# Moving the token gathers behind the scatters, and reordering the first expert's weight splits, in a fused attention and mixture-of-experts kernel

## The chip, the cores and the metric

The kernel runs on one core of a Trainium2 chip. The metric is the time of one execution on the device in microseconds (us). The kernel before takes 622.65 us, the median of three runs that lie between 622.59 and 622.91 us.

The core's engines run their own instruction streams and meet through semaphores: PE (TensorE, matrix products and transposes), DVE (VectorE), ACT (ScalarE), POOL (GpSimd) and SP (SyncE, here used to start transfers). POOL also starts the indirect transfers, those whose rows are chosen by an index tile.

## The reference

Attention over 4 batches, 8 heads, 576 positions and 64 features per head, with a bias that a small network makes from the distance of two positions, is followed by a mixture of experts over the 2304 tokens of 512 features. Each token goes to the one expert with the largest gate logit.

```python
scores = scale * np.matmul(q, k.transpose(0, 1, 3, 2)) + bias        # bias: relu(x @ w1 + b1) @ w2 per head
attn = softmax(scores)
x = np.matmul(attn, v).transpose(0, 2, 1, 3).reshape(2304, 512)
...
e_idx = np.argmax(x @ w_gate, axis=1)
for e in range(8):
    mask = e_idx == e
    h = np.maximum(x[mask] @ w1[e], 0.0)                              # 512 -> 1024
    out[mask] = gate_w[mask, None] * eom[mask, e, None] * (h @ w2[e]) # 1024 -> 512
```

## The kernel before

**Stages.** The bias tiles are built first; then sixteen pairs of heads are worked through, with tables of short codes (`ORDER`, `FIRST`, `LAST`, `END`) that fix the order of the work of each pair. Finished token rows are written to a tensor `x_dram` in HBM. The routing of the first three batches is done before the experts begin, that of the fourth batch is spread through the first five expert slots (`SLOT_WORK`).

**Slots.** The expert stage works in slots of 288 tokens of one expert, `body(s)` for s = 0 to 7; more slots, and a short one of 32 tokens, follow from the routing. A slot has two loops on PE. The f loop makes 8 blocks of 128 hidden columns, each from 12 products (L1115). The d loop makes 4 blocks of 128 output columns, each from 24 products (L1138). Each float32 operand is held as a high part and a remainder, so a weight has to be split: ACT copies the high part and the remainder is a subtraction. In the slots the subtraction is DVE's (`split`, L486 and L487). For slot 0 it is POOL's (`first_split`, L539 and L540), in eight halves: half i belongs to weight chunk i // 2 and holds columns 0 to 511 or 512 to 1023, which serve blocks 0 to 3 and 4 to 7 of the f loop. The code `y` in the table `LAST` takes one entry of the list `splits`.

**Tokens.** `gather(s)` (L497) fetches the 288 rows of a slot in three indirect transfers of 96 rows into the tiles `xg`, of which there are two sets, for even and odd slots. After blocks 1 and 2 of the d loop of slot s, `transpose_x(s + 1, c)` (L515 to L517) turns the next slot's rows. At a slot's end the answer is turned (L1157), copied (L1160), and `put` (L1080) writes it with three indirect transfers, the scatters.

**Order on POOL.** POOL runs its instructions in the order in which the program lists them, and an instruction that waits holds up those behind it. The gather for slot s + 2 is listed in slot s between the two loops, ahead of the scatters of slot s; it waits until the transposes of slot s have read its tile set. `gather(0)` stands in `first_x` (code `X`), `gather(1)` behind all of the attention. The short slot's rows are fetched by `gather(FIRST_FEW)` and turned by `transpose_few` (L505) ahead of the d loop of slot 7.

**Transfers on SP.** `load_w1(s)` (L478) and `load_w2(s)` (L483) fetch an expert's weights, four transfers each, and each waits until the splits have read the buffer that it fills. `load_w1(1)` is listed behind the eighth half of `first_split`.

Of the kernel before, what the change touches and what calls it, by code (L numbers as in the profile page):

```python
# [134 lines left out]
def attention_moe_kernel(  # L135
# [49 lines left out]
    def psum_t():  # L185
        return ps_t.tile([128, 512], F32, name="pt", tag="t")
# [284 lines left out]
    def expert(s):  # L471
        at = 2 * ns + 1 if s == FIRST_FEW else s
        return nc.values_load(seq[int(s >= SURE_A)][0:1, at:at + 1], engines=(EV.SP,), min_val=0, max_val=NE - 1)

    def load_w1(s):
        src = mw1[bass.ds(expert(s), 1)].rearrange("o (c p) f -> p (o c) f", p=128)
        for i in range(4):
            nc.sync.dma_start(out=w1r[i], in_=src[:, i, :])  # L478

    def load_w2(s):  # L480
        src = mw2[bass.ds(expert(s), 1)].rearrange("o (c p) f -> p (o c) f", p=128)
        for i in range(4):
            nc.sync.dma_start(out=w2r[i], in_=src[:, 2 * i:2 * i + 2, :])  # L483

    def split(hi, lo, src):
        nc.scalar.copy(out=hi, in_=src)  # L486
        V.tensor_tensor(out=lo, in0=src, in1=hi.bitcast(F32), op=ALU.subtract)  # L487

    def side(s):

        return s % 2 if s < SURE else 0

    def gather(s):
        part = int(s >= SURE_A)
        for j in range(1 if s == FIRST_FEW else 3):
            g = 3 * s + j
            nc.gpsimd.indirect_dma_start(  # L497
                out=xg[side(s)][j], out_offset=None, in_=x_dram[:, :] if part else x_dram[0:(B - 1) * S, :],
                in_offset=bass.IndirectOffsetOnAxis(ap=gidx[part][:, g:g + 1], axis=0),
            )  # L500

    def transpose_few():
        pt = psum_t()
        for c in range(4):
            nc.tensor.transpose(  # L505
                pt[:, c * G:c * G + G], xg[0][0][:, c * 128:c * 128 + 128], ident[0:G, 0:G]
            )
        V.tensor_copy(out=few[0], in_=pt[:, 0:4 * G].rearrange("p (c g) -> p c g", g=G)[:, :, 0:FEW])

    def transpose_x(s, c):  # L510
        xh, xl = xs[side(s)]
        xg_s = xg[side(s)]
        pt = psum_t()
        for j in range(3):
            nc.tensor.transpose(pt[:, j * G:j * G + G], xg_s[j][:, c * 128:c * 128 + 128], ident[0:G, 0:G])  # L515
        nc.scalar.copy(out=xh[:, c, :], in_=pt[:, 0:CH])
        V.tensor_tensor(out=xl[:, c, :], in0=pt[:, 0:CH], in1=xh[:, c, :].bitcast(F32), op=ALU.subtract)  # L517
        if s >= SURE:
            V.tensor_copy(out=few[0][:, c, :], in_=pt[:, 0:FEW])
# [13 lines left out]
    def first_split(i):  # L533
        if i == 0:
            for m, to in enumerate((w1h, w1l)):
                t = biasp.tile([128, 4, DFF], F32R, name=f"w1_{m}", tag=f"bias{m}")
                to.extend(t[:, c, :] for c in range(4))
        c, h = i // 2, slice(i % 2 * 512, i % 2 * 512 + 512)
        nc.scalar.copy(out=w1h[c][:, h], in_=w1r[c][:, h])  # L539
        nc.gpsimd.tensor_tensor(  # L540
            out=w1l[c][:, h], in0=w1r[c][:, h], in1=w1h[c][:, h].bitcast(F32), op=ALU.subtract
        )
        if i == 7:
            load_w1(1)

    def first_w2():
        t = biasp.tile([128, 4, 2, DM], F32, name="w2r", tag="bias3")
        w2r.extend(t[:, i] for i in range(4))
        load_w2(0)
# [122 lines left out]
    with ExitStack() as actx:  # L672
# [316 lines left out]
            f(*a)  # L989

        chunks = [0, 1, 2, 3]
        splits = list(range(8))

        def copies(c):
            return nc.scalar.copy if c == "a" else V.tensor_copy
# [5 lines left out]
        for n in range(len(pairs) + 1):  # L1001
            todo = {i: 1 for i in range(8)}
            for op in orders.get(n, ORDER).split():
# [21 lines left out]
                i = int((name + "0")[1])  # L1025
# [30 lines left out]
                        finish(emit_kq(b, pr, i))  # L1056
                else:
                    {"l": emit_load, "v": emit_load_v, "c": emit_z, "b": emit_load_vb, "g": emit_zb, "z": emit_q4}[name](b, pr)
        gather(1)
        while chunks:  # L1060
            transpose_x(0, chunks.pop(0))

    with ExitStack() as ctx:
# [14 lines left out]
        def put(s, j, y, n=G):  # L1078
            idx = sidx[int(s >= SURE_A)][0:n, 3 * s + j:3 * s + j + 1]
            p = nc.gpsimd.indirect_dma_start(  # L1080
                out=out, out_offset=bass.IndirectOffsetOnAxis(ap=idx, axis=0),
                in_=y[0:n], in_offset=None, bounds_check=NTOK - 1, oob_is_err=False,
            )
            for other in puts:
                tc.declare_no_dep(p.ins, other.ins, reason="no row of the answer is written twice")
            puts.append(p)
# [4 lines left out]
        def new_y(s, j):  # L1091

            if s == SURE - 1:
                return xg[1][j]
            return y2 if j == 2 else x_p.tile([128, DM], F32, name="y", tag="x")[0:G]

        def slot_work(s, at):
            for w in SLOT_WORK[s].split() if s < len(SLOT_WORK) else ():
                if w == at:
                    do_work()  # L1100

        def after(s, n):

            return None if s >= SURE else s + n if s + n < SURE else FIRST_FEW if s + n == SURE else None

        def body(s):
            assert s < 5 or not (work or rows)
            xh, xl = xs[side(s)]
            for f in range(8):
                fs = slice(f * 128, f * 128 + 128)  # L1110
                p1 = ps1.tile([128, 512], F32, name="p1", tag="p1")
                n = 0
                for c in range(4):
                    for w, x in ((w1h[c], xh), (w1h[c], xl), (w1l[c], xh)):
                        nc.tensor.matmul(p1[:, 0:CH], lhsT=w[:, fs], rhs=x[:, c, :], start=n == 0, stop=n == 11)  # L1115
                        n += 1
                nc.scalar.activation(out=hh[f], in_=p1[:, 0:CH], func=ACTF.Relu)  # L1117
                V.scalar_tensor_tensor(
                    out=hl[f], in0=p1[:, 0:CH], scalar=0.0, in1=hh[f].bitcast(F32), op0=ALU.max, op1=ALU.subtract
                )  # L1120
                if f % 2 == 0:
                    i = f // 2
                    split(w2h[i], w2l[i], w2r[i])
                slot_work(s, "f%d" % f)
            if after(s, 1):
                load_w2(after(s, 1))
            if after(s, 2):
                gather(after(s, 2))
            yt = yts[s % 2]
            if after(s, 1) == FIRST_FEW:  # L1130
                transpose_few()
            for d in range(4):
                ds = slice(d * 128, d * 128 + 128)
                p2 = ps2.tile([128, 512], F32, name="p2", tag="p2")
                n = 0
                for f in range(8):
                    for w, x in ((w2h, hh), (w2h, hl), (w2l, hh)):
                        nc.tensor.matmul(  # L1138
                            p2[:, 0:CH], lhsT=w[f // 2][:, f % 2, ds], rhs=x[f], start=n == 0, stop=n == 23
                        )  # L1140
                        n += 1
                if after(s, 1) == s + 1:
                    split(w1h[d], w1l[d], w1r[d])
                nc.scalar.copy(out=yt[:, d, :], in_=p2[:, 0:CH])
                if after(s, 1) == s + 1 and d in (1, 2):
                    for c in (2 * d - 2, 2 * d - 1):
                        transpose_x(s + 1, c)
                if after(s, 1) == FIRST_FEW and d < 3:
                    (few_hidden, few_turn, few_last)[d]()
                slot_work(s, "d%d" % d)  # L1150
            if after(s, 2):
                load_w1(after(s, 2))
            pts = [psum_t() for j in range(3)]
            for d0, d1 in ((0, 3), (3, 4)):
                for j, pt in enumerate(pts):
                    for d in range(d0, d1):
                        nc.tensor.transpose(pt[0:G, d * 128:d * 128 + 128], yt[:, d, j * G:j * G + G], ident)  # L1157
            for j, pt in enumerate(pts):
                y = new_y(s, j)
                (V.tensor_copy, nc.scalar.copy, V.tensor_copy)[j](out=y, in_=pt[0:G, :])  # L1160
                if s != SURE - 1:
                    put(s, j, y)

        few_h, few_ht = (yts[0].rearrange("p a b -> p (a b)")[:, 256 * i:256 * i + 256] for i in range(2))

# [51 lines left out]
        for s in range(SURE):  # L1217
            body(s)
# [44 lines left out]
```

## Time and profile before

| what | us |
|---|---|
| median of three runs | 622.65 |
| the profiled execution | 615.56 |
| its span, first to last instruction | 613.4 |
| PE busy in the span | 575.6 |
| DVE busy | 413.5 |
| ACT busy | 374.8 |
| POOL busy | 94.9 |
| mean granted clock of PE | 0.987 of full speed |

The profile is one execution. A timeline lists instructions in order of time, with the idle time of the engine ahead of each and what ended it in brackets. The chain is followed back from the last instruction to what released each step. A landing is the time from the issue of a transfer until its data has arrived. "Busy x" in a table by stage is busy microseconds and instruction count. The experts' slot 0 begins at 370.2 us, slot 1 at 401.7, slot 2 at 431.6, slot 3 at 459.5, slot 4 at 488.0, slot 5 at 515.9, slot 6 at 543.8 and slot 7 at 571.7.

### The profile page before, as it was taken

The numbers are of one execution on the slowest core, as the hardware profiler recorded it, in microseconds if no ns is written. First come the engines' busy times: TensorE is split into PE (matmuls) and PEld (weight loads), VectorE is DVE, ScalarE is ACT, GpSimd is POOL, SyncE is SP. The second block draws the span as 40 slices with busy tenths as digits, with TensorE's granted clock in tenths as the row PEclk, the third lists the DMA queues.
The fourth block names the chain that finished last, engine by engine and source line by source line (L and its number), as shares of the span: only waits on it lengthen the run. The fifth ranks groups of instructions, "written<-read, shape, count | busy, mean of one in ns | idle before, by whom it ended". The sixth has DMA issues, their size and how long they took to land.

```text
span 613.4 us, 13534 instructions
## 1 busy us (share of the span) xinstructions
PE 575.6 (94%) x5070; PEld 489.3 (80%) x5070; DVE 413.5 (67%) x974; ACT 374.8 (61%) x774; POOL 94.9 (15%) x172
## 2 busy tenths in 40 slices
PE   4878789999999999999999999999999999999993
PEld 2333478887887788887778769999999999999993
DVE  6968656676786677786579765766777675555621
ACT  5778667777775677776776664545545454545410
POOL 1000000000001000100012383040404132220202
PEclk9979989999999999999999999999999999999998
DMA  6998975655656745676436686576656574855521
GB/s 144 226 207 207 215 161 116 139 125 108 143 127 169 167 99 108 137 184 157 105 88 158 185 263 198 172 221 204 202 179 203 172 221 145 241 166 182 174 71 47
DMA packets 99094, 100.26 MB, mean 163 GB/s; under 512 B 71320, under 2 KB 71576, under 8 KB 99017
## 3 DMA queue, kind: packets, MB, share of 16 engines
q1 hardware_dynamic: 93028, 84.93, 54.4%
q0 software_dynamic: 3232, 9.64, 5.0%
q10 hardware_dynamic: 2756, 4.72, 2.2%
q8 instruction: 42, 0.69, 0.5%
q14 instruction: 36, 0.29, 0.2%
HBM read 60.34 MB, written 9.50 MB: 114 GB/s over the span
## 4 chain that ended last, share of the span: by engine, by line
PE 79%; DVE 7%; ACT 5%; DMA 5%; issue 3%; POOL 0%; POOLq 0%; SPq 0%; DVEq 0%; ACTq 0%
PE p L1115 16%; PE p L1138 16%; PE pa L922 13%; PE ps L853 10%; PE pt L890 10%; PE pt L803 2%; DMA bias<-evh 2%; PE pb L735 2%; PE ps L869 2%; DVE e L833 2%; DVE hid L724 2%; PE pt L655 1%; PE pt L1157 1%; PE pt L902 1%; PE pt L515 1%
## 5 line engine op out<-in xcount | busy, mean ns | idle before, releaser
L838 ACT ACTIVATE e<-e,nm 128x576 f32<-128x576 f32 x144 | 111.2, 773 | 49.1 <-DVE nm L833 47.0
L833 DVE CUSTOM_DVE_ANT_0 e<-ps,bias 128x576 f32<-128x576 f32 x144 | 105.6, 751 | 31.3 <-PE ps L853 25.3
L1115 PE MATMUL p<-x,w 128*128 128x288 f32 x768 | 105.8, 297 | 0.0
L1115 PEld LDWEIGHTS p<-x,w 128*128 128x128 f32 x768 | 102.8, 188 | 0.5 <-issue 0.4
L890 PE MATMUL pt<-kept,e 128*128 128x128 f32 x576 | 82.7, 277 | 2.9 <-ACT et L894 1.6
L853 PE MATMUL ps<-qt,qs 128*128 128x288 f32 x256 | 79.9, 331 | 3.2 <-DVE nm L833 3.0
L890 PEld LDWEIGHTS pt<-kept,e 128*128 128x128 f32 x576 | 65.2, 141 | 17.8 <-issue 7.0
L1138 PE MATMUL p<-hh,w2h 128*128 128x288 f32 x256 | 77.4, 302 | 0.0
L1138 PE MATMUL p<-hl,w2h 128*128 128x288 f32 x256 | 75.7, 296 | 0.1
L1138 PE MATMUL p<-hh,w2l 128*128 128x288 f32 x256 | 75.4, 295 | 0.0
L922 PE MATMUL pa<-et,vt 128*64 128x256 f32 (+1 forms) x640 | 73.2, 354 | 0.0
L853 PE MATMUL ps<-kl,qs 128*128 128x288 f32 x256 | 71.3, 296 | 0.0
L894 ACT COPY et<-pt 128x512 f32<-128x512 f32 (+1 forms) x105 | 57.2, 565 | 12.4 <-PE pt L890 12.3
L735 PE MATMUL pb<-hid,w2blk 128*32 128x288 f32 x576 | 47.8, 442 | 17.3 <-DVE hid L724 7.4
L922 PEld LDWEIGHTS pa<-et,vt 128*64 128x64 f32 x640 | 42.6, 137 | 21.8 <-issue 6.0
L853 PEld LDWEIGHTS ps<-qt,qs 128*128 128x128 f32 x256 | 48.9, 191 | 7.2 <-DVE nm L833 4.5
L1117 ACT ACTIVATE hh<-p 128x288 fp32r<-128x288 f32 x64 | 26.3, 411 | 46.1 <-PE p L1115 38.0
L1080 POOL DMA_INDIRECT out_dram<-y,sidx x22 | 26.4, 1198 | 172.9 <-DVE y L1160 145.3
L735 PEld LDWEIGHTS pb<-hid,w2blk 128*32 128x32 f32 x576 | 19.1, 116 | 42.1 <-DVE hid L724 10.7
L724 DVE TENSOR_SCALAR hid<-e,early 128x576 f32<-128x576 f32 x110 | 48.4, 511 | 6.1 <-PE pb L735 2.8
L853 PEld LDWEIGHTS ps<-kl,qs 128*128 128x128 f32 x256 | 49.1, 192 | 0.0
L487 DVE TENSOR_TENSOR w2l<-w2r,w2h 128x1024 fp32r<-128x1024 f32 x32 | 39.2, 1225 | 14.5 <-ACT w2h L486 14.5
(218 smaller groups left out, 970.8 us busy)
## 6 DMA issues: line engine op xcount, KB each, us to landing
w1r<-in_moe_w_dram SPq DMA_DIRECT2D x36, 512.0 KB, 3.7
w2r<-in_moe_w_dram SPq DMA_DIRECT2D x36, 512.0 KB, 4.0
kl<-qs SPq DMA_DIRECT2D x32, 288.0 KB, 5.2
nat<-in_k_dram SPq DMA_DIRECT2D x16, 288.0 KB, 3.9
nat<-in_q_dram SPq DMA_DIRECT2D x16, 288.0 KB, 5.2
bias<-evh SPq DMA_DIRECT2D x16, 288.0 KB, 4.2
bias<-evl SPq DMA_DIRECT2D x16, 288.0 KB, 5.3
qs<-qt SPq DMA_DIRECT2D x16, 288.0 KB, 3.2
```

The source lines that it names most:

```text
L487: V.tensor_tensor(out=lo, in0=src, in1=hi.bitcast(F32), op=ALU.subtract)
L724: V.tensor_scalar(out=to, in0=src, scalar1=bc[:, r:r + 1], scalar2=0.0, op0=ALU.add, op1=ALU.max,)
L735: nc.tensor.matmul(pb[32 * t:32 * t + 32, c, 0:288], lhsT=w2f, rhs=hids[t][:, c * 288:c * 288 + 288], start=True, stop=True,)
L833: V.tensor_tensor_reduce(out=e.rearrange("p (a j) -> p a j", a=2), in0=ps[:, :, 0:n], in1=bias_ap.rearrange("p (a j) -> p a j", a=2), scal ...
L838: nc.scalar.activation(out=e, in_=e, func=ACTF.Exp, scale=-1.0, bias=nm, accum_out=sum_ap)
L853: nc.tensor.matmul(ps[:, c, 0:288], lhsT=qs[:, o:o + 128], rhs=keys[:, k0 + c * 288:k0 + c * 288 + 288], start=n == 0, stop=n == 1,)
L890: nc.tensor.transpose(pt[:, n * 256 + j * 128:n * 256 + j * 128 + 128], es[j][:, (n0 + n) * 128:(n0 + n) * 128 + 128], ident,)
L894: copy(out=et[:, n0:n0 + nn, :].rearrange("p n s -> p (n s)"), in_=pt[:, 0:nn * 256])
L922: nc.tensor.matmul(pa[p:p + 64, 0:n], lhsT=values, rhs=weights, start=i == 0, stop=i == 4)
L1080: p = nc.gpsimd.indirect_dma_start(out=out, out_offset=bass.IndirectOffsetOnAxis(ap=idx, axis=0), in_=y[0:n], in_offset=None, bounds_check ...
L1115: nc.tensor.matmul(p1[:, 0:CH], lhsT=w[:, fs], rhs=x[:, c, :], start=n == 0, stop=n == 11)
L1138: nc.tensor.matmul(p2[:, 0:CH], lhsT=w[f // 2][:, f % 2, ds], rhs=x[f], start=n == 0, stop=n == 23)
```

## The change

Three things are edited. In the list `splits` the four halves with the low columns come first. `gather(1)` moves from the end of the attention into `first_split`, behind the half with number 6, which is now the fourth of eight. In `body` the gather for two slots ahead moves from between the two loops to the end, behind the scatters of the slot.

```diff
--- before.py
+++ after.py
@@ -542,6 +542,8 @@
         )
         if i == 7:
             load_w1(1)
+        elif i == 6:
+            gather(1)
 
     def first_w2():
         t = biasp.tile([128, 4, 2, DM], F32, name="w2r", tag="bias3")
@@ -989,7 +991,7 @@
             f(*a)
 
         chunks = [0, 1, 2, 3]
-        splits = list(range(8))
+        splits = [0, 2, 4, 6, 1, 3, 5, 7]
 
         def copies(c):
             return nc.scalar.copy if c == "a" else V.tensor_copy
@@ -1056,7 +1058,6 @@
                         finish(emit_kq(b, pr, i))
                 else:
                     {"l": emit_load, "v": emit_load_v, "c": emit_z, "b": emit_load_vb, "g": emit_zb, "z": emit_q4}[name](b, pr)
-        gather(1)
         while chunks:
             transpose_x(0, chunks.pop(0))
 
@@ -1124,8 +1125,6 @@
                 slot_work(s, "f%d" % f)
             if after(s, 1):
                 load_w2(after(s, 1))
-            if after(s, 2):
-                gather(after(s, 2))
             yt = yts[s % 2]
             if after(s, 1) == FIRST_FEW:
                 transpose_few()
@@ -1160,6 +1159,8 @@
                 (V.tensor_copy, nc.scalar.copy, V.tensor_copy)[j](out=y, in_=pt[0:G, :])
                 if s != SURE - 1:
                     put(s, j, y)
+            if after(s, 2):
+                gather(after(s, 2))
 
         few_h, few_ht = (yts[0].rearrange("p a b -> p (a b)")[:, 256 * i:256 * i + 256] for i in range(2))
```

The first place is POOL's list from the second split of slot 0 to the last of its gathers. `w_1` is the remainder of the first w1, `w1r_4425` to `w1r_4428` are the four raw chunks, `xg_4653` takes the first two parts of an even slot's rows, `xg_4654` the third part, and all three of an odd slot's. Before, from the second split (chunk 0's high columns) on:

```order
L540 TENSOR_TENSOR w_1_4595<-w1r_4425,w_0_4594 128x512
L540 TENSOR_TENSOR w_1_4595<-w1r_4426,w_0_4594 128x512
L497 DMA xg_4653<-x_dram,gidx_102 96x512 x2
L497 DMA xg_4654<-x_dram,gidx_102 96x512
L540 TENSOR_TENSOR w_1_4595<-w1r_4426,w_0_4594 128x512
L540 TENSOR_TENSOR w_1_4595<-w1r_4427,w_0_4594 128x512 x2
L540 TENSOR_TENSOR w_1_4595<-w1r_4428,w_0_4594 128x512 x2
L497 DMA xg_4654<-x_dram,gidx_102 96x512 x3
L497 DMA xg_4653<-x_dram,gidx_102 96x512 x2
L497 DMA xg_4654<-x_dram,gidx_102 96x512
```

After, from the second split (chunk 1's low columns) on:

```order
L540 TENSOR_TENSOR w_1_4595<-w1r_4426,w_0_4594 128x512
L540 TENSOR_TENSOR w_1_4595<-w1r_4427,w_0_4594 128x512
L497 DMA xg_4653<-x_dram,gidx_102 96x512 x2
L497 DMA xg_4654<-x_dram,gidx_102 96x512
L540 TENSOR_TENSOR w_1_4595<-w1r_4428,w_0_4594 128x512
L497 DMA xg_4654<-x_dram,gidx_102 96x512 x3
L540 TENSOR_TENSOR w_1_4595<-w1r_4425,w_0_4594 128x512
L540 TENSOR_TENSOR w_1_4595<-w1r_4426,w_0_4594 128x512
L540 TENSOR_TENSOR w_1_4595<-w1r_4427,w_0_4594 128x512
L540 TENSOR_TENSOR w_1_4595<-w1r_4428,w_0_4594 128x512
```

The three gathers of slot 1 now stand behind four splits and ahead of the four others; the three gathers of slot 2 have left this stretch, and stand behind the first three scatters.

The second place is POOL's list in slots 3 to 5. `out_dram` rows are scatters, `gidx_102` is the index tile of the first six slots and `gidx_103` that of the later ones. Before, from the scatters of slot 3 to the first gathers of slot 7:

```order
L1080 DMA out_dram<-y,sidx_104 2304x512 x2
L1080 DMA out_dram<-y_4858,sidx_104 2304x512
L497 DMA xg_4653<-x_dram,gidx_103 96x512 x2
L497 DMA xg_4654<-x_dram,gidx_103 96x512
L1080 DMA out_dram<-y,sidx_104 2304x512 x2
L1080 DMA out_dram<-y_4858,sidx_104 2304x512
L497 DMA xg_4654<-x_dram,gidx_103 96x512 x3
```

After, from the scatters of slot 3 to the first gathers of slot 6:

```order
L1081 DMA out_dram<-y,sidx_104 2304x512 x2
L1081 DMA out_dram<-y_4858,sidx_104 2304x512
L497 DMA xg_4654<-x_dram,gidx_102 96x512 x3
L1081 DMA out_dram<-y,sidx_104 2304x512 x2
L1081 DMA out_dram<-y_4858,sidx_104 2304x512
L497 DMA xg_4653<-x_dram,gidx_103 96x512 x2
L497 DMA xg_4654<-x_dram,gidx_103 96x512
```

Between two groups of scatters there are three gathers in both, but for the slot one earlier now: the scatters of slot 3 were followed by the gathers of slot 6 (the first with `gidx_103`, which the routing in slot 4 fills), and are now followed by those of slot 5.

## Rows read from the trace of the kernel before

**Rows 1.** The page: chain that ended last, share of the span by engine.
```profile
PE 79%; DVE 7%; ACT 5%; DMA 5%; issue 3%; POOL 0%; POOLq 0%; SPq 0%; DVEq 0%; ACTq 0%
```

**Rows 2.** Busy time by stage (columns named in the first row).
```profile
core 0: us, PE busy (x) PEld busy (x) DVE busy (x) ACT busy (x) POOL busy (x), PEclk, DMA share, GB/s
345.00:370.00 25.00, 23.09 (x224) 17.54 (x224) 17.07 (x47) 15.53 (x38) 16.57 (x18) 1.00 0.79 261
370.20:401.70 31.50, 31.29 (x250) 29.93 (x249) 21.09 (x51) 14.16 (x29) 4.10 (x5) 1.00 0.58 183
...
515.90:543.80 27.90, 27.90 (x218) 27.89 (x218) 16.01 (x23) 14.16 (x26) 7.17 (x6) 1.00 0.64 191
```

**Rows 3.** Chain in order of time, fifth to last slot: start us, us, what.
```profile
515.89 12.80 PE p L1115 x96
...
535.09 0.50 PE pt L515 x6
...
584.54 0.33 PE pt L505 x4
```

**Rows 4.** POOL in order of time, around slot 0's start: start us, us, instruction [idle before].
```profile
355.70 2.64 POOL L540 TENSOR_TENSOR w<-w1r,w 128x512 fp32r<-128x512 f32 x2 [1.54 <-ACT w L539]
358.49 1.03 POOL L497 DMA_INDIRECT xg<-x_dram,gidx  x1 [0.16 <-DVE et L894]
...
361.99 6.22 POOL L540 TENSOR_TENSOR w<-w1r,w 128x512 fp32r<-128x512 f32 x5
368.37 0.91 POOL L497 DMA_INDIRECT xg<-x_dram,gidx  x1 [0.16 <-issue]
```

**Rows 5.** ACT in order of time: its fourth split copy.
```profile
358.48 0.60 ACT L539 CAST w<-w1r 128x512 fp32r<-128x512 f32 x1
```

**Rows 6.** PE in order of time: start of slot 0, its fourth and fifth column blocks.
```profile
370.19 1.86 PE L1115 MATMUL p<-x,w 128*128 128x288 f32 x12
...
376.70 3.47 PE L1115 MATMUL p<-x,w 128*128 128x288 f32 x24
```

**Rows 7.** First expert's four w1 loads alone: landing.
```profile
DMA to landing us min/median/max: 3.6/5.3/6.8
```

**Rows 8.** SP's queue in order of time: w1 and w2 loads.
```profile
344.78 2.44 SPq L478 DMA_DIRECT2D w1r<-in_moe_w_dram  x4
...
357.01 11.56 SPq L478 DMA_DIRECT2D w1r<-in_moe_w_dram  x4
374.76 4.49 SPq L483 DMA_DIRECT2D w2r<-in_moe_w_dram  x2
```

**Rows 9.** ACT in order of time: first split of the second expert's w1.
```profile
388.50 1.03 ACT L486 CAST w<-w1r 128x1024 fp32r<-128x1024 f32 x1
```

**Rows 10.** All 25 gathers (L497): duration, landing.
```profile
L497 POOL DMA_INDIRECT xg<-x_dram,gidx x25: 909/932/1668, 358.5 to 549.1; - x25
...
DMA to landing us min/median/max: 3.0/5.0/7.9
```

**Rows 11.** DMA issues, the gather of 549.14 alone: landing in us.
```profile
xg<-x_dram,gidx POOLq DMA_INDIRECT x1, 3.9
```

**Rows 12.** POOL in order of time, slots 4, 5 and 7.
```profile
496.88 0.93 POOL L497 DMA_INDIRECT xg<-x_dram,gidx  x1 [3.88 <-PE p L1115]
...
522.48 1.67 POOL L497 DMA_INDIRECT xg<-x_dram,gidx  x1 [0.30 <-PE p L1115]
524.45 0.92 POOL L497 DMA_INDIRECT xg<-x_dram,gidx  x1 [0.30 <-issue]
...
574.98 1.80 POOL L1080 DMA_INDIRECT out_dram<-y,sidx  x1 [0.31 <-issue]
```

**Rows 13.** DVE in order of time, the stretch of the gather of 522.48.
```profile
522.11 1.23 DVE L487 TENSOR_TENSOR w2l<-w2r,w2h 128x1024 fp32r<-128x1024 f32 x1 [0.48 <-ACT w2h L486]
```

**Rows 14.** DVE in order of time, first w2 split of slot 0.
```profile
373.51 1.23 DVE L487 TENSOR_TENSOR w2l<-w2r,w2h 128x1024 fp32r<-128x1024 f32 x1 [0.41 <-ACT w2h L486]
```

## The prediction

> **What bounds the kernel now.** I read the chain by engine first, then the busy time by stage, then the chain in order of time through the slots, and only then POOL, the one engine whose list changes. The chain lies on PE for 79% of the span, and POOL, POOL's queue and SP's queue round to 0% [rows 1]. The stages say it more sharply: in slot 5 PE is busy for 27.90 of 27.90 us, at a granted clock of 1.00 [rows 2]; slots 2, 3, 4 and 6 read the same. There a transfer that arrives earlier can give nothing, and one that arrives later costs only what it comes after the moment at which PE asks for it. The stretch before slot 0 (345 to 370) has 25.00 - 23.09 = 1.91 us of PE idle, and slot 0 has 31.50 - 31.29 = 0.21 us [rows 2]. Those 2.12 us are the most that an edit around them could win back.
>
> **Part one: low halves first.** POOL makes a remainder in 6.22 / 5 = 1.24 us [rows 4]. Before, three stand ahead of the gathers of slot 0 and five behind, and the eighth ends at 361.99 + 6.22 = 368.21. After, three low halves stand ahead, the fourth low half ends at 361.99 + 1.24 = 363.23. PE's first product of slot 0 starts at 370.19 without idle time ahead of it [rows 6]: it came straight from its own attention work and found all eight remainders there. So having the low ones 3.7 us sooner (before, the last low half was the seventh, done at 368.21 - 1.24 = 366.97) gains 0.
>
> ACT's list keeps as many copies at the same points, but the fourth, at 358.48 [rows 5], now reads the fourth chunk of w1. Its load is issued by 344.78 + 2.44 = 347.22 [rows 8] and lands within 6.8 us [rows 7], so by 354.0. Cost 0, cover 4.5 us; were it gone, ACT would wait with the attention's exponentials queued behind the copy.
>
> **Part two: slot 1's gathers among the splits.** Three gathers repeat every 1.21 to 1.33 us: the group of slot 0 fills 358.49 to 361.99, 3.5 us, and the next group starts 0.16 us behind a split [rows 4]. After: fourth low half until 363.23, three gathers until about 363.23 + 0.16 + 3.6 = 367.0, four high halves until 367.0 + 4 x 1.24 = 372.0. The high halves are first read by the fifth block of the f loop. Blocks four and five start at 376.70 and together take 3.47 us [rows 6], so the fifth starts at about 378.4. Cover 6.4 us, cost 0. Behind the late splits on POOL stand only the scatters of slot 0, which come at the slot's end. Slot 1's rows are turned in the d loop of slot 0, later than ACT's 388.50 [rows 9], so fetching them 5 us earlier gains nothing.
>
> SP is touched too. The four loads of the second w1 were issued as the splits released the chunks, over 357.01 to 368.57 [rows 8]. Now every chunk is held until its high half is done, so the issues fall at 368.3, 369.5, 370.8 and 372.0. With the 6.8 us of [rows 7] the last lands by 372.0 + 0.4 + 6.8 = 379.2, and ACT first reads a chunk at 388.50 [rows 9]: cover 9 us, cost 0. Behind them on SP's queue waits the second w2 at 374.76 [rows 8], 2.4 us after the last w1 issue and released by DVE's split that ends at 373.51 + 1.23 = 374.74 [rows 14], so it does not move. Moving 2 MB away from the gathers of slot 0 may bring those sooner, but PE shows no wait for them.
>
> **Part three: gathers behind scatters.** The waiting moves, the traffic hardly does. Already before, a gather listed ahead of the scatters ran as soon as its index and tiles were free: right behind the scatters of the slot before, as at 522.48 and 524.45 in slot 5 [rows 12]. There stood the gather for slot 7 while slot 5 ran; now the gather for slot 6 stands there. The lead shrinks from more than a slot to the length between scatter and transpose, and the one gather that held up POOL, that of 496.88 with 3.88 us of idle [rows 12], no longer does; no one waited behind it. In slot 5 the third gather starts at 524.45 and the transposes at 535.09 [rows 3, 12]: 10.6 us, against landings of 3.0 to 7.9 us, median 5.0 [rows 10]. Cover 2.7 us at the slowest landing. Six gathers (slots 2 to 7) stand so, cost 0.
>
> The short slot's gather is the tightest. It was at 549.14 and comes now behind the scatter of 574.98, which takes 1.80 us [rows 12], so at about 577.1. PE turns its rows at 584.54 [rows 3]: 7.4 us. A single gather behind three scatters landed in 3.9 us [rows 11]; I take that, 581.0, cost 0. By the extremes of [rows 10] it lands between 580.1 and 585.0, so its cost lies between 0 and 0.5 us.
>
> **Sum.** 0 + 0 + 0, with 0.5 us above and 2.1 us below as ends: the profiled execution would stay at 615.56. It is 7.1 us shorter than the median of the runs; I carry the difference over unchanged and forecast 622.65.
>
> **A rule against the change.** The gather of 522.48 took 1.67 us where the median is 0.93 [rows 10, 12], and DVE's remainder of w2, with both inputs in SBUF, ran from 522.11 to 523.34 [rows 13]: POOL lost about as much as the overlap, 0.86 us. The Trainium skill, SBUF — State Buffer, "Who interferes with whom", says that such a DVE instruction and a GpSimd one that reads SBUF exclude each other for a whole instruction, whichever starts first. By that rule the later high halves could hold DVE up in slot 0, which is the second rival below; this trace shows the loss on POOL's side only.
>
> **Rivals.**
> 1. Rows come late to a transpose, so the kernel is slower. For: the lead is now 10.6 us, and 7.4 us for the short slot, and the timed runs are 7.1 us longer than the profile somewhere. Against: none of 25 landings passed 7.9 us. It decides from 8.7 us for the short slot (577.1 + 8.7 - 584.54 = 1.26 us) or from 10.8 us in all six (0.2 us each). At landings of 12 us it costs 6 x 1.4 + 4.6 = 13 us: 635.7. At 7.9 us it costs 0.5: 623.1.
> 2. POOL's high halves run into DVE's first remainder of w2 at 373.51 [rows 14] and hold it for up to 1.24 us each, twice at most, 2.5 us: 625.1. It needs the splits 1.5 us later than 372.0. For: 0.74 us of excess on the long gather. Against: DVE has no such instruction between 363 and 372. Even seven POOL instructions with 0.74 us more end at 377.2, still ahead of the fifth block.
> 3. The stretch before slot 0 tightens, since 2 MB of loads leave it and POOL's pieces move. At most 1.91 us: 620.7. Against: PE's idle there ends on ACT's and DVE's softmax and copies, none of which is moved.
>
> **How the numbers follow.** Forecast 0.78, late rows 0.08, blocked DVE 0.04, tighter start 0.08, and 0.02 for causes I do not see that stay small. A measurement of this kernel tells 0.2% from no change, that is 1.25 us. Forecast and the 0.02 are "same", 0.80; the third rival is "faster", 0.08; the first two are "slower", 0.12. The range, 621.5 to 623.9, takes in the 0.5 us of the short slot and half of what the tighter start could give, and leaves out rivals at their full price.
>
> **What would show it.** Right: POOL's list with four splits ending near 372, PE from 370 to 571 with no new wait, the transposes of slots 2 to 7 and of the short slot without idle time ahead of them, the second w1's loads issued between 368 and 373. Wrong: idle on PE at L515 or L505 released by a gather, DVE's remainders in slot 0 above 1.23 us, or an idle time of PE before slot 0 that is clearly off 1.9 us.

## The result and the profile after

The changed kernel takes 616.16 us (median of 6 runs, 614.06 to 616.63). The kernel before takes 622.49 us beside it (6 runs, 620.66 to 622.91). The medians differ by 6.3 us, where I forecast no change; the ratio is 0.9914, with a 95% interval of 0.9891 to 0.9937, which stands for 5.4 us. The forecast of 622.65 us and its range, 621.5 to 623.9, both miss.

The profiled execution of the changed kernel took 616.42 us with a span of 614.5. That is not shorter than the profiled execution before (615.56, span 613.4). So the two profiles, laid side by side, show no gain at all, and the timed runs show 6.3 us. This contradiction is what the experiments are for.

First the profile after, view by view. The chain by engine, against [rows 1]:

```profile
PE 79%; DVE 7%; DMA 5%; ACT 4%; issue 3%; POOL 0%; POOLq 0%; SPq 0%; DVEq 0%; ACTq 0%
```

Busy time by stage, against [rows 2] (stretches shifted so that each begins where its stage begins):

```profile
core 0: us, PE busy (x) PEld busy (x) DVE busy (x) ACT busy (x) POOL busy (x), PEclk, DMA share, GB/s
345.00:371.50 26.50, 23.85 (x231) 17.98 (x229) 17.43 (x49) 15.87 (x38) 17.44 (x19) 1.00 0.69 225
371.56:403.00 31.44, 31.22 (x249) 29.86 (x249) 21.02 (x50) 14.15 (x29) 0.55 (x1) 1.00 0.57 183
517.20:545.10 27.90, 27.90 (x218) 27.89 (x217) 16.01 (x23) 14.20 (x25) 7.17 (x6) 1.00 0.62 195
```

Slot 5 is full as before, and slot 0 has 0.22 us of PE idle where it had 0.21. POOL's busy time in slot 0 is 0.55 us in place of 4.10. And ahead of slot 0, PE is idle for 26.50 - 23.85 = 2.65 us where it was 1.91. POOL in order of time shows why its number changed, against [rows 4]:

```profile
361.38 0.91 POOL L497 DMA_INDIRECT xg<-x_dram,gidx  x1 [0.31 <-issue]
362.30 1.30 POOL L540 TENSOR_TENSOR w<-w1r,w 128x512 fp32r<-128x512 f32 x1
363.76 0.91 POOL L497 DMA_INDIRECT xg<-x_dram,gidx  x1 [0.16 <-issue]
...
366.19 0.91 POOL L497 DMA_INDIRECT xg<-x_dram,gidx  x1 [0.31 <-issue]
367.13 4.99 POOL L540 TENSOR_TENSOR w<-w1r,w 128x512 fp32r<-128x512 f32 x4
```

Slot 1's three gathers end at 367.10, the splits at 372.12, and no gather follows until slot 0's scatters. The idle time of PE ahead of slot 0 grew behind slot 0's own gathers (358.81 to 362.29): there DVE waits longer for PE than before. DVE in order of time, after and before:

```profile
363.17 0.42 DVE L925 COPY xt<-pa 128x256 f32<-128x256 f32 x1 [2.62 <-PE pt L588]
```

```profile
361.86 0.43 DVE L923 COPY xt<-pa 128x256 f32<-128x256 f32 x1 [1.63 <-PE pa L922]
```

The change does not move these gathers, and e1 shows the same wait (2.64 us) in the kernel before. SP's queue, against [rows 8]: the second w1's loads go out from 368.44 to 372.47.

```profile
368.44 4.03 SPq L478 DMA_DIRECT2D w1r<-in_moe_w_dram  x4
376.08 4.51 SPq L483 DMA_DIRECT2D w2r<-in_moe_w_dram  x2
```

The chain in order of time (start us, us, what; L1116 is the f loop that was L1115), against [rows 3, 6]: slot 0's first and fourth blocks, slot 1's first, the short slot's transposes, and the chain's last scatter.

```profile
371.56 1.79 PE p L1116 x12
...
378.10 3.41 PE p L1116 x24
...
403.06 3.19 PE p L1116 x24
...
585.87 0.33 PE pt L505 x4
...
606.70 0.92 POOL out_dram L1081
```

The same landmarks in the kernel before, rows not shown yet:

```profile
370.26 1.79 PE p L1115 x12
...
401.73 3.19 PE p L1115 x24
...
605.36 0.92 POOL out_dram L1080
```

Such distances are the most useful reading here. From slot 1's first product to the chain's last scatter it is 606.70 - 403.06 = 203.64 us after and 605.36 - 401.73 = 203.63 before. So moving the gathers in slots 1 to 7 neither costs nor gives anything. Slot 0 takes 403.06 - 371.56 = 31.50 and 401.73 - 370.26 = 31.47. The 1.3 us by which slot 0 starts later lie in the stretch ahead of it, and they are not the change's: the same kernel, profiled again, started slot 0 at 371.27, and in e12, which differs from it only from slot 3 on, at 370.24.

**How to read the times.** Kernels of one series of runs ran on one chip, in turn with the kernel before. Series came in two kinds, and no number below can be read without that. In the series of the result and in those of e1 to e4 and e9 to e12 the kernel before takes 620.8 to 622.5 us; I call these long series. In the four others it takes 615.2 to 615.4 us. It is not the chip: the chip of e9 to e12 was that of e16 and e17. The profile of before that the prediction reads (615.56) agrees with the second kind, the three times beside it (622.65) with the first.

### The profile page after: what moved, and what is told of

Same layout as the page of the kernel before. It is cut to its first block, busy times and chain, and to the rows that moved or that the text cites. A ratio compares the mean times of both kernels' runs of the same rounds, so it can differ in the third digit from the quotient of the medians.

```text
span 614.5 us, 13532 instructions
## 1 busy us (share of the span) xinstructions
PE 575.9 (94%) x5070; PEld 489.2 (80%) x5070; DVE 413.7 (67%) x974; ACT 375.0 (61%) x774; POOL 96.1 (16%) x172
## 4 chain that ended last, share of the span: by engine, by line
PE 79%; DVE 7%; DMA 5%; ACT 4%; issue 3%; POOL 0%; POOLq 0%; SPq 0%; DVEq 0%; ACTq 0%
PE p L1116 16%; PE p L1137 16%; PE pa L924 13%; PE ps L855 10%; PE pt L892 9%; PE pb L737 2%; DVE hid L726 2%; PE pt L805 2%; PE ps L871 2%; DMA bias<-evh 2%; DVE e L835 2%; PE pt L657 1%; PE pt L1156 1%; PE pt L904 1%; PE pt L515 1%
## 5 line engine op out<-in xcount | busy, mean ns | idle before, releaser
L1116 PE MATMUL p<-x,w 128*128 128x288 f32 x768 | 105.9, 297 | 0.0
L1116 PEld LDWEIGHTS p<-x,w 128*128 128x128 f32 x768 | 102.8, 188 | 0.5 <-issue 0.4
L487 DVE TENSOR_TENSOR w2l<-w2r,w2h 128x1024 fp32r<-128x1024 f32 x32 | 39.2, 1226 | 14.2 <-ACT w2h L486 12.7
```

## The experiments

**Theories.** A: the rows land earlier, or a stage is tighter, all over the kernel. B: something at slot 0's start costs the kernel before some 6 us, in series of one kind only, and the profile of before was taken in one without it. Within B, either the order of the splits ends it, or the loads of the second w1, or the six gathers that stand in a row.

**e1, the kernel before once more, unchanged.**

> The kernel before, unchanged, against itself. Theory M (the kernel before has two kinds of execution, and the profiled one of 615.6 us was the rare kind while the timed ones near 622 us lose some 6 us at one place): both sides of the comparison lie near 621 to 623 us, with now and then one near 615, and a span and clock per run show whether the 6 us go with a lower granted clock of PE. Theory C (a difference of chips or of the hour): both sides near 615 to 616 us.

620.99 us against 620.82 (ratio 1.0005, 0.9984 to 1.0027), span 618.1: a profile of the long kind. None of the 35 runs is below 618.8 us, so the two kinds do not mix here as theory M of the expectation had it, and the granted clock does not tell them apart: 0.990 in this profile, 0.987 in the first. POOL in order of time at slot 0's start:

```profile
368.10 0.91 POOL L497 DMA_INDIRECT xg<-x_dram,gidx  x1 [0.16 <-issue]
369.31 0.91 POOL L497 DMA_INDIRECT xg<-x_dram,gidx  x1 [0.30 <-issue]
370.53 0.91 POOL L497 DMA_INDIRECT xg<-x_dram,gidx  x1 [0.30 <-issue]
371.74 0.91 POOL L497 DMA_INDIRECT xg<-x_dram,gidx  x1 [0.30 <-issue]
372.96 0.91 POOL L497 DMA_INDIRECT xg<-x_dram,gidx  x1 [0.30 <-issue]
374.18 0.91 POOL L497 DMA_INDIRECT xg<-x_dram,gidx  x1 [0.31 <-issue]
```

Six gathers without a break, slot 1's and slot 2's. The first profile of before has the same six, 368.37 to 375.53. PE makes the last products of a tile of the attention, DVE copies that tile (L923), ACT applies the first activation of slot 0 (L1117), and here is when. PE, DVE and ACT in order of time, and the chain:

```profile
370.75 0.29 PE L922 MATMUL pa<-et,vz 128*64 128x64 f32 x4
```

```profile
376.76 0.22 DVE L923 COPY xt<-pa 128x64 f32<-128x64 f32 x1 [4.96 <-remote]
```

```profile
377.12 0.41 ACT L1117 ACTIVATE hh<-p 128x288 fp32r<-128x288 f32 x1 [5.80 <-remote]
```

```profile
371.32 5.73 another core or an unknown queue
...
379.23 1.58 PE p L1115 x12
...
406.32 3.19 PE p L1115 x24
...
609.91 0.92 POOL out_dram L1080
```

And the first profile of before at the same two instructions, DVE first:

```profile
370.49 0.21 DVE L923 COPY xt<-pa 128x64 f32<-128x64 f32 x1
```

```profile
372.13 0.41 ACT L1117 ACTIVATE hh<-p 128x288 fp32r<-128x288 f32 x1 [2.12 <-issue]
```

The copy runs 0.52 us after PE's product starts there (370.49 - 369.97), and 6.01 us after it here (376.76 - 370.75). The activation runs 1.94 us after the start of slot 0's first block there, and 6.16 us here (377.12 - 370.96). "Another core" is the profile's word for a wait that no recorded update ends. The trace's records of PE's semaphore updates agree: none between 370.90 and 376.74, then ten within 0.4 us. In the first profile the same updates come from 371.13 on, 0.13 us apart. So these updates were held back and came all at once. From PE's first product of slot 0 (370.96; before, 370.19 [rows 6]) to slot 1's first it is 406.32 - 370.96 = 35.36 us, where the first profile has 401.73 - 370.19 = 31.54: 3.8 us lost. From there to the chain's last scatter it is 203.59, as in the profiles before and after. Ahead of slot 0 DVE's copy behind slot 0's own three gathers waits 2.64 us here, 1.63 in the first profile, and PE is idle for 0.8 us more. The 3.8 and the 0.8 make up the 4.7 us by which the span is longer (618.1 against 613.4). Theory A falls here: the loss sits at these two rows of gathers, and most of it at slot 0's start.

**e2, the new order of the splits alone.**

```
-        splits = list(range(8))
+        splits = [0, 2, 4, 6, 1, 3, 5, 7]
```

> Only the order of the eight halves is changed (low halves first). If the 6 us of the timed runs of before are lost because the first columns of the first w1 come late, this gives about 616 us, ratio 0.99. If the gathers are what counts: ratio 1.00, 622 us.

623.44 us, ratio 1.0024 (1.0002 to 1.0046). No gain, if anything a small loss. POOL still has six in a row, and ACT waits the same way:

```profile
377.19 0.41 ACT L1117 ACTIVATE hh<-p 128x288 fp32r<-128x288 f32 x1 [6.35 <-issue]
```

**e3, slot 1's gathers moved alone** (behind the fourth split, in the old order).

```
         if i == 7:
             load_w1(1)
+        elif i == 3:
+            gather(1)
...
-        gather(1)
         while chunks:
```

> Only the gathers of slot 1 are moved, behind the fourth of the eight halves in their old order; the later halves end 3.6 us later. If the 6 us hang on when the rows of slot 1 come, or on when the loads of the second w1 start: ratio 0.99. Otherwise 1.00.

616.53 us, ratio 0.9926 (0.9908 to 0.9945): the whole gain, as far as the intervals tell. POOL now has three and three, with 4.98 us of splits between. Slot 2's group still stands in slot 0. ACT in order of time there:

```profile
372.71 0.41 ACT L1118 ACTIVATE hh<-p 128x288 fp32r<-128x288 f32 x1 [2.12 <-issue]
...
375.86 0.41 ACT L1118 ACTIVATE hh<-p 128x288 fp32r<-128x288 f32 x1 [1.53 <-PE pt L618]
```

**e4, the gathers behind the scatters alone** (slot 1's where they were).

```
-            if after(s, 2):
-                gather(after(s, 2))
             yt = yts[s % 2]
...
                     put(s, j, y)
+            if after(s, 2):
+                gather(after(s, 2))
```

> Only the gathers of two slots ahead are moved behind the scatters. If the 6 us are lost where POOL waits with the gathers of slot 6 in slot 4, or by the gathers of slot 2 beside slot 0's start: ratio 0.99, 616 us. If the splits or slot 1's gathers count: 1.00, 622 us.

616.59 us, ratio 0.9931 (0.9911 to 0.9951): the whole gain too. Either half of the change is enough, because either parts the six. Three gathers are left at slot 0's start, and DVE's copy with them. POOL, then DVE:

```profile
367.17 0.91 POOL L497 DMA_INDIRECT xg<-x_dram,gidx  x1 [0.16 <-issue]
...
369.60 0.91 POOL L497 DMA_INDIRECT xg<-x_dram,gidx  x1 [0.30 <-issue]
```

```profile
371.62 0.23 DVE L923 COPY xt<-pa 128x64 f32<-128x64 f32 x1 [0.72 <-PE p L1115]
```

The copy is late here as well: 1.82 us after its product (369.80), so 1.3 us late. It starts 1.1 us after the third gather ended at 370.51, as it started 1.7 us after the sixth in e1 (375.09 to 376.76). In e3 the second activation starts 1.0 us after that row's end (374.87 to 375.86). The hold-up thus lasts a little longer than the row. PE's updates show it here too: none between 369.98 and 371.60, then nine within 0.3 us. Three gathers at this place cost nothing in slot 0, since ACT's first activation has to wait for PE's first block anyway (it starts 1.96 us after the block here, 371.98 - 370.02, and 1.94 us in the first profile), and PE runs on meanwhile; six outlast that cover.

**e5 to e8, in a series of the other kind.** e5 sets a POOL copy that waits for slot 0's last activation ahead of slot 2's gathers; e6 leaves the second expert's w1 unloaded; e7 leaves four in a row; e8 is the changed kernel with three needless gathers behind those at slot 3's end, so six in a row there.

```
+        spacer = hp.tile([64, 64], F32, name="spacer")
...
+            if s == 0:
+                nc.gpsimd.tensor_copy(out=spacer, in_=hh[7][0:64, 0:64].bitcast(F32))
             if after(s, 2):
                 gather(after(s, 2))
```

> The kernel before with one small POOL copy ahead of the gathers of slot 2 in slot 0, which waits for the last block of the f loop, so that the two groups of three gathers no longer stand next to each other; all else in its old place. Theory B (six gathers in a row hold up the semaphore updates of the other engines for some 5.7 us at the start of slot 0): about 616 us, ratio 0.992, and no wait of ACT at L1117 above 2.2 us there. Theory L (the loads of the second w1 beside the gathers do it) and theory S (something else at slot 0's start): 621 us, ratio 1.00.

```
-        if i == 7:
-            load_w1(1)
```

> The kernel before without the four loads of slot 1's w1 (slot 1 is computed with slot 0's w1), the six gathers in a row as they were. Theory B: the wait of 5 to 6 us stays, 621 us, though it may begin some us sooner since nothing is ahead of the gathers in the transfer engines. Theory L: the wait goes, 616 us or less.

```
-    def gather(s):
+    def gather(s, js=(0, 1, 2)):
...
-        for j in range(1 if s == FIRST_FEW else 3):
+        for j in (0,) if s == FIRST_FEW else js:
...
-                gather(after(s, 2))
+                gather(after(s, 2), (0,) if s == 0 else (0, 1, 2))
...
+            if s == 0:
+                gather(2, (1, 2))
```

> The kernel before with four gathers in a row at slot 0's start instead of six: the second and the third of slot 2 stand behind the scatters of slot 0. Theory B by length of the burst: a shorter wait, 617 to 619 us. A threshold at more than four: 616 us. Theory S: 621 us.

```
             if after(s, 2):
                 gather(after(s, 2))
+            if s == 3:
+                for j in range(3):
+                    nc.gpsimd.indirect_dma_start(
+                        out=xg[0][j], out_offset=None, in_=x_dram[0:(B - 1) * S, :],
+                        in_offset=bass.IndirectOffsetOnAxis(ap=gidx[0][:, j:j + 1], axis=0),
+                    )
```

> The changed kernel with three needless gathers behind those at the end of slot 3, into a token tile that is free there, so that six gathers stand in a row beside slot 4's f loop. Theory B anywhere: updates are held up for 5 to 6 us there too, PE waits some 3 to 5 us, 619 to 621 us, ratio to the kernel before about 0.998 (against 0.992 without them). Theory S (only slot 0's start is open to it): 616 us, ratio 0.992.

The kernel before takes 615.21 us here. Ratios: e5 1.0016 (0.9999 to 1.0034), e6 0.9995 (0.9975 to 1.0016), e7 1.0006 (0.9982 to 1.0030), e8 1.0008 (0.9994 to 1.0022). Nothing tells them apart, since nothing is held up in this series: e6 has six gathers in a row (366.41 to 373.57), and its ACT waits 2.11 us for the first activation (2.12 in the first profile). Where the expectations speak of a difference, they were written with the long kind in mind, and miss. What the series does show: without the hold-up the change is worth nothing, since e8, which holds all of it, takes 615.30. (The changed kernel without the needless gathers was not run in such a series.)

**e9 to e12, the changed kernel and three of these again, in a long series** (before 622.46).

> The changed kernel again, to be read by the time that the kernel before has on the same chip. So far the kernel before took 620.8 us on one chip and 615.2 on another, whose traces differ in one more thing: on the first some 480 of 5418 records of transfers' semaphore updates are missing. Theory K (chips differ; on the slow kind six gathers in a row hold up semaphore updates): ratio 0.992 where the kernel before takes 621, and 1.00 where it takes 615. If the gain is the change's own on every chip: 0.992 in both cases.

> The kernel before with the POOL copy that parts the two groups of gathers, again. Where the kernel before takes 615 us: 1.00 and nothing is learned. Where it takes 621: theory B (six in a row) 616 us, ratio 0.992; theories L and S 621 us, 1.00.

> The kernel before without the loads of slot 1's w1, again (slot 1 is computed with slot 0's w1). Where the kernel before takes 621: theory B keeps the wait, 620 to 621 us, ratio 1.00; theory L loses it, 615 us, 0.991. Where it takes 615: 1.00.

> The changed kernel with three needless gathers behind those at the end of slot 3, again. Where the kernel before takes 621: if six in a row hold up the updates anywhere, 619 to 621 us, ratio 0.998; if slot 0's start is special, 616 us, 0.992. Where it takes 615: 1.00.

e9: 616.05, ratio 0.9925 (0.9898 to 0.9953); the result repeats.

e10: 616.56, ratio 0.9923 (0.9898 to 0.9948). Nothing of the change is in it but that slot 2's gathers leave the row, behind one small copy. ACT waits 2.11 us for the first activation. With e3, where slot 1's gathers leave the row and slot 2's stay, this is the plainest evidence that the row of six is the cause: either three alone are free in slot 0.

e11, without the second expert's w1: 622.84, ratio 0.9999 (0.9970 to 1.0028). The loads are not the cause. Queues and issues from 366 to 380 us (packets, MB, share): the gathers' queue q0 moves alone but for two packets of instructions, and the wait is there all the same, for ACT longer than in e1.

```profile
q0 software_dynamic: 384, 1.18, 31.5%
q8 instruction: 1, 0.02, 0.6%
q14 instruction: 1, 0.01, 0.2%
xg<-x_dram,gidx POOLq DMA_INDIRECT x6
```

```profile
376.12 0.22 DVE L921 COPY xt<-pa 128x64 f32<-128x64 f32 x1 [3.21 <-PE pt L584]
```

```profile
379.15 0.41 ACT L1115 ACTIVATE hh<-p 128x288 fp32r<-128x288 f32 x1 [6.80 <-issue]
```

DVE's copy was let go in the middle of the row here (the sixth gather ends at 377.49), 3.81 us after its product; the activation came 1.7 us behind the row's end, 6.63 us after its block's start at 372.52.

e12, six in a row behind slot 3's scatters: 616.04, ratio 0.9915 (0.9891 to 0.9938). This cost nothing. POOL in order of time (L1166 are the needless ones):

```profile
493.29 0.94 POOL L497 DMA_INDIRECT xg<-x_dram,gidx  x1 [0.30 <-issue]
...
497.73 1.66 POOL L1166 DMA_INDIRECT xg<-x_dram,gidx  x1 [0.30 <-issue]
...
500.92 1.67 POOL L1166 DMA_INDIRECT xg<-x_dram,gidx  x1 [0.30 <-PE p L1116]
```

So six in a row do not hold up the kernel wherever they stand. It is not that a delay is covered here; there is none. ACT takes a block from PE every 1.60 us throughout, after the same idle time as in e9, which lacks the needless gathers. ACT in e12, then in e9:

```profile
499.19 0.41 ACT L1118 ACTIVATE hh<-p 128x288 fp32r<-128x288 f32 x1 [1.19 <-PE p L1116]
```

```profile
500.22 0.41 ACT L1118 ACTIVATE hh<-p 128x288 fp32r<-128x288 f32 x1 [1.19 <-PE p L1116]
```

Three of the six took 1.66 or 1.67 us here, so they are spread over 9.3 us where e1's took 7.0, and PE is in the middle of its f loop. Which of the two, or what else, keeps the updates in time was not tried.

**e13, e14 and e16 to e19, four and five gathers in a row, three times.**

The edit of four is that of e7; that of five differs from it in this:

```
...
-                gather(after(s, 2))
+                gather(after(s, 2), (0, 1) if s == 0 else (0, 1, 2))
...
+            if s == 0:
+                gather(2, (2,))
```

> The kernel before, but with only the first of slot 2's three gathers where it was; the other two stand behind slot 0's scatters. So four gathers stand in a row at the start of slot 0, where the kernel before has six and the changed one three. If what holds up the semaphore updates grows with the number of gathers in the row, then on a chip where the kernel before takes about 622 us this one takes some 618 to 620 us and its trace shows a wait of 1 to 4 us at the start of slot 0. If three and four are both too few, it takes about 616 us (ratio 0.992). If the cause is not the length of the row, it stays at about 622 us. On a chip where the kernel before takes about 615 us all give no difference.

> The same with two of slot 2's gathers left where they were, so that five stand in a row. If the hold-up grows with the row, this is between the run with four and the kernel before (about 619 to 621 us where the kernel before takes 622 us). If there is a threshold, it is at 616 us or at 622 us and nothing between. On a chip where the kernel before takes about 615 us, no difference.

> The kernel with four gathers in a row at the start of slot 0 again, in the hope of a chip on which the kernel before takes about 622 us. There: 618 to 620 us and a wait of 1 to 4 us at the start of slot 0 if the hold-up grows with the row; 616 us if four are too few; 622 us if the length of the row is not the cause. On a chip where the kernel before takes about 615 us, no difference.

> The kernel with five gathers in a row again. Where the kernel before takes about 622 us: 619 to 621 us if the hold-up grows with the row, 616 or 622 us and nothing between if there is a threshold. On a chip where the kernel before takes about 615 us, no difference.

> Four gathers in a row at the start of slot 0, a third time. The chip of the last two runs had before taken 622.5 us for the kernel before and took 615.4 us now, so what makes the loss appear belongs to the session and not to the chip. In a session where the kernel before takes about 622 us: 618 to 620 us if the hold-up grows with the row, 616 us if four are too few, 622 us if the length of the row is not the cause. In one where it takes 615 us: no difference, and the trace holds all records of semaphore updates (8151).

> Five gathers in a row, a third time. Where the kernel before takes about 622 us: 619 to 621 us if the hold-up grows with the row, 616 or 622 us and nothing between if there is a threshold. Where it takes 615 us: no difference.

All three series were of the other kind (before 615.31, 615.44, 615.15). Ratios with four: 1.0001 (0.9981 to 1.0020), 0.9999 (0.9976 to 1.0022), 1.0008 (0.9996 to 1.0020). With five: 1.0001 (0.9982 to 1.0019), 1.0007 (0.9994 to 1.0020), 0.9991 (0.9977 to 1.0005). They do not answer their question, at what length the row starts to cost time; what stands on it are three (free in slot 0) and six (3.8 us in e1, more in e2 and e11).

They do add that the kind goes with the series, and with its records. With nothing left out of the kernel, the traces of the other kind hold 8147 to 8196 records of semaphore updates, the first profile of before among them (8151); those of the long series hold 7617 to 7811, that of the changed kernel among them (7659). Whether the recording itself holds the updates up, or whatever loses the records also delays the updates, stays open: every run here was recorded.

## Why the prediction was wrong

**The step that failed** stands right behind the sum: "It is 7.1 us shorter than the median of the runs; I carry the difference over unchanged and forecast 622.65." The 7.1 us were not an offset between a profile and a clock. They were, for the greater part, a stall at slot 0's start that the timed runs had and the profiled one had not (3.8 us in e1, 5.8 in e11), and the stall was the very thing that the change takes away. The first rival used those 7.1 us as a hint that the runs might be longer "somewhere", and the forecast should have asked where: 7 us that no view shows are a term of their own, with a chance of going away.

**Part one, 0.** No gain, as forecast: the reordered splits alone give 1.0024, just above the noise on the slow side.

**Part two, 0.** Its mechanics came as written: splits until 372.12 (forecast 372.0), loads at 368.44 to 372.47 (368.3 to 372.0), and the second w2 behind them no later against slot 0's start (376.08 - 371.56 = 4.52; before, 374.76 - 370.26 = 4.50). It was 0 in the kind of execution that the rows came from, and alone it is the whole gain in the other (e3).

**Part three, 0.** The text says that before, a gather ran "right behind the scatters of the slot before". That holds for slots 3 to 7, not for slot 2's three, ahead of which no scatter stood: they ran at 372.02 to 375.53, in one row with slot 1's. POOL's list of before, in the section on the change, shows the six one behind the other, but my rows with times ended at 368.37, with the first of them. So the row of six was in view, and its cost was put at nothing with no times read for it; no rival and no bound speaks of it. For the other slots the step was right. In slot 5 the last gather starts at 525.78 and the transposes at 536.42, 10.6 us later, as forecast; the short slot's gather starts at 578.41 and is needed at 585.87, 7.5 us later (forecast 7.4), and PE does not wait. POOL in order of time, against [rows 12]:

```profile
523.82 1.66 POOL L497 DMA_INDIRECT xg<-x_dram,gidx  x1 [0.31 <-PE p L1116]
525.78 0.92 POOL L497 DMA_INDIRECT xg<-x_dram,gidx  x1 [0.30 <-issue]
...
578.41 0.94 POOL L497 DMA_INDIRECT xg<-x_dram,gidx  x1 [0.30 <-issue]
```

**The ends of the sum.** "2.1 us below" came from PE's idle time in the profiled execution. In e1 the same stretch, slot 0, holds 3.8 us more. A bound read from an execution binds only executions like it. The sign that I named as wrong, "an idle time of PE before slot 0 that is clearly off 1.9 us", did come, with 2.65 us, but it is not the change's: in the same stretch e1, the kernel before, has 2.67 and e12, which holds the whole change, has 1.91.

**The rivals.** Late rows, blocked DVE and a tighter start did not happen. Between DVE and POOL the loss was on POOL's side alone again: one gather of slot 5, started at 523.82 while DVE's remainder ran from 523.44 to 524.67, took 1.66 us. All 60 of DVE's two-input remainders in the changed kernel kept their length (groups of L487: duration ns min/median/max, first and last start):

```profile
L487 DVE TENSOR_TENSOR w2l<-w2r,w2h x32: 1224/1226/1226, 374.8 to 585.7; 128x1024 fp32r<-128x1024 f32 x32
L487 DVE TENSOR_TENSOR w<-w1r,w x28: 1203/1226/1228, 390.9 to 570.1; 128x1024 fp32r<-128x1024 f32 x28
```

**What stays open.** The profiles show 3.8 us (e1), 5.3 (e2, 36.84 us from slot 0 to slot 1) and 5.8 (e11, 37.35 us) lost in slot 0, beside the 4.2 to 6.4 us by which the versions without the row beat the kernel before in long series; why the size differs was not tried. PE itself falters in e1: the second block of slot 0 starts at 374.38 and its last six products at 376.71, after idle time that nothing in the profile ends, so the late updates may not be the whole of it. The changed kernel in long series (616.1) stays 0.9 us above the 615.2 of the others. In the result's profile PE is idle for 0.7 us more behind slot 0's own gathers (2.65 against 1.91 us), a row of three that no version here parted; e12's profile does not have this idle time, so how much of the 0.9 us it makes up is not shown. No version run here is clearly faster than the changed one.

## What to carry to other kernels

If the profiled execution is clearly shorter than the timed runs, it is not a picture of them: profile the kernel again, and lay distances between the same landmarks side by side, before any forecast is added to it. Look at what stands in a row on a queue across the parts of a program, since two groups written a hundred lines apart may run back to back. Where such a row stands at a place at which other engines wait for each other, try it parted: here one small copy between the two groups (e10) gave the whole gain. That the row would cost as much elsewhere is not shown; beside slot 4's f loop it cost nothing (e12).

## What the runs showed of the hardware

A row of six indirect gathers on POOL, with nothing but 0.3 us between them, came with semaphore updates of PE that reached their waiters late: DVE's copy by 5.5 us and ACT's activation by 4.2 us in e1, by 3.3 and 4.7 us in e11, where no other transfer of data moved. With three in a row DVE's copy was 1.3 us late (e4), and behind slot 0's own three it waited 1.0 us longer (the result's profile). When the hold-up ended, PE's updates came some 0.04 us apart (ten within 0.4 us in e1), where the first profile has them 0.13 us apart. None of this is tied to the row alone. It showed in some series only, and one chip had series of both kinds (e9 to e12, e16 and e17); e6 has six in a row and no wait. Six in a row beside slot 4's f loop delayed nothing (e12). None of it shows as a busy engine either: DVE and ACT stand idle and PE in part, and the late start of a short copy (0.22 us, 6.0 us after its product) is what tells of it.
